# One head's V in six-row loads with 192 keys, norms that turn y as it stands, query ahead of the variance, gates in two PSUM tiles

## The chip, the cores and the metric

The kernel runs on one core of a Trainium2 chip. The metric is device time in microseconds for one execution, the median of several runs. The core has TensorE (PE in the profile, with its weight loads as PEld), VectorE (DVE), ScalarE (ACT), GpSimd (POOL) and SyncE (SP), which here issues nearly all transfers from HBM. Sixteen DMA engines carry those transfers.

## What is computed

Four decode positions (B = 4, width D = 640) go through two kinds of layer twice: attention over a cache, then a gated MLP. All data are float32.

```python
# A: W = max(256, Sk // 4) = 1024 of the 4096 cached keys, 32 heads of 128
q = (layernorm(x) @ wq) -> (B, 32, 1, 128)
p = softmax(q . k[:, :, -1024:] * 128 ** -0.5)
x = x + (p . v[:, :, -1024:]) @ wo
# B: F = 1728
gate, up = layernorm(x) @ W_gate, layernorm(x) @ W_up
x = x + (gate * (gate > 0) * up) @ W_down
# A and B once more, with the same weights and caches
```

`_layernorm` is `(x - mean) / sqrt(var + 1e-5)`, without scale or shift. Keys and values of one head are 2 x 4 x 1024 x 128 floats, 4 MB; both passes over attention need the 32 heads' K, V, query and output weights.

## The kernel before

**Memory.** One SBUF tile `store` of 50,304 columns holds everything that is loaded, as a ring that is filled by a plan made when the program is built. Host code lays weights and caches out as wide rows of 128 partitions: `heads` (most heads' q, k, o and v in the order of use), `kept` (the last two groups of heads, which stay in SBUF from the first attention to the second), `mlp`, and `limbs`. `plan` is a list of loads in order; `load()` (L226) issues the next ones on SP's queue as long as their place in `store` is free (`live`), and `done()`/`free()` mark columns as free once the products that read them are issued, and call `load()` again. A big load of `heads` has up to `MOST` = 16,064 columns, 64,256 B in each partition; three of them make a lap of the ring.

**Limbs.** V of a head is eight blocks of 512 columns (128 keys for the 4 positions each). Head 17 (`SPLIT`) has only seven in the `heads` row. The eighth block's 128 keys come in small loads of the `limbs` row: `LIMBS` (L74) lists eight loads of five rows by 1536 columns, three of two rows and two of one row by 512 columns. The rows of a load are four partitions apart. They land in the last `PART` = 2048 columns of `store`, on partitions 0 to 63. `RUNS` (L75) says which keys lie where. `stretch()` (L144) puts them into the plan: one ahead of the third last big load before the head's V, six ahead of the next and six ahead of the last. In `values()` (L463) seven small matmuls (L476) move the probabilities of those keys to the partitions where the rows landed, DVE copies them (L485), and seven matmuls with 20 or 8 rows (L490) add the products.

**Norms.** `y` is one PSUM tile that carries x through all four layers: position b of quarter g of the width stands on partition 32 g + b. `normalized()` (L376): DVE sums y (L381), ScalarE copies it to SBUF (L382), four matmuls with `sel_q` spread the mean (`mean`, L374), DVE subtracts (L385), ScalarE squares with a sum (L386), and DVE transposes in 32 x 32 blocks to `xT` (L388). `deviation()` turns the sum of squares into 1/sqrt on ScalarE and DVE (L394, L395). `query()` (L408) multiplies `xT` with one group's query weights in five parts of the width.

**MLP.** `forward()`: `gate(3)`, then gates 0 to 2 with `hidden()` and `gated()` between them, then the `down()` products into y. The gate products of all four parts go to the two halves of PSUM tile `pp`. `busy` (transposes) and `fill` (matmuls) issue work of no use for the result (L358, L365) while `waits[0]` is set, which is so in the norms and, in the first pass, through the MLP.

**Order.** The instructions of each engine run in the order of the program; nothing reorders them (`manual_schedule`). SP works its issues off in order too: an issue that waits for a place, or for the earlier DMA with its semaphore, holds those behind it.

Of the kernel before, what the change touches and what calls it, by code (L numbers as in the profile page):

```python
# [9 lines left out]
AF = mybir.ActivationFunctionType  # L10
# [63 lines left out]
LIMBS = [(half + i, 5, 0, 1536) for i in range(4) for half in (0, 32)] + [(i, 2, 1536, PART) for i in range(3)] + [(3, 1, 1536, PART), (7, 1, 1536, PART)]  # L74
RUNS = [(half, 20, 512 * s, 40 * s + 20 * (half > 0)) for s in range(3) for half in (0, 32)] + [(0, 8, 1536, 120)]  # L75


def size_of(what, i):
    if what == "v" and i == SPLIT:
        return KV - 512  # L80
    return len(HEADS[i]) * D if what == "q" else D if what == "o" else KV
# [32 lines left out]
def decode_kernel(ctx: ExitStack, tc: tile.TileContext, x, source, out):  # L114
# [29 lines left out]
    def stretch(layer, lo, end, to):  # L144

        loads = []
        for hi in fewest(lo, end, -(-(end - lo) // MOST))[1]:
            if to + hi - lo > LAP:
                to = 0
            loads.append((lo, hi, to))  # L150
            to, lo = to + hi - lo, hi
        last = next(i for i, (lo, hi, _) in enumerate(loads) if lo < at_part("v", SPLIT) + KV - 512 <= hi)
        for i, (lo, hi, at) in enumerate(loads):
            if last - 3 < i <= last:
                half = (i - last + 1) * 6 + 1
                plan.extend((layer, "limbs", p, p + 1, STORE - PART) for p in range(max(half, 0), half + 6))
            put(layer, "heads", at, lo, hi)
        return to
# [67 lines left out]
    def load():  # L226

        if not held:
            nc.sync.dma_start(out=first_q, in_=source["heads"][:, :HELD])
        while plan:  # L230
            layer, row, lo, hi, to = plan[-1]
            if any(live[to:STORE if row == "limbs" else to + hi - lo]):
                break
            plan.pop()
            if row == "limbs":
                live[to:STORE] = [lo == len(LIMBS) - 1] * PART
                p, n, a, b = LIMBS[lo]
                nc.sync.dma_start(out=store[p:p + 4 * n - 3:4, to + a:to + b], in_=source[row][p:p + 4 * n - 3:4, a:b])  # L238
                continue
            live[to:to + hi - lo] = [True] * (hi - lo)  # L240
            held.setdefault((layer, row), []).append((lo, hi - lo, to))
            nc.sync.dma_start(out=store[:, to:to + hi - lo], in_=source[row][:, lo:hi])
# [111 lines left out]
    def busy(n):  # L354

        if waits[0]:
            for _ in range(n):
                nc.tensor.transpose(po[:, :P], ident, ident)  # L358
# [18 lines left out]
    def normalized():  # L377

        ysb, xc, sq = probs[:, :QUARTER], gates[:, :QUARTER], gates[:, QUARTER:2 * QUARTER]
        waits[0] = True  # L380
        nc.vector.tensor_reduce(su, y, axis=AX.X, op=ALU.add)  # L381
        nc.scalar.copy(ysb, y)  # L382
        busy(2)
        mu = mean(su)
        nc.vector.tensor_tensor(xc, ysb, mu.to_broadcast([P, QUARTER]), op=ALU.subtract)  # L385
        nc.scalar.activation(sq, xc, AF.Square, accum_out=ss)  # L386
        fill(1)
        nc.vector.transpose(xT, xc)  # L388
        return ss
# [18 lines left out]
    def query(layer, g, spread=False):  # L408
# [7 lines left out]
        part_done(layer, "q", g, 0, (KC - 1) * n)  # L416
        c = KC - 1
# [4 lines left out]
        part_done(layer, "q", g, c * n, n)  # L422

# [39 lines left out]
    def values(layer, g, last=False):  # L463
# [3 lines left out]
        for i, h in enumerate(HEADS[g]):  # L467
# [3 lines left out]
            whole = 7 if h == SPLIT else 8  # L471
            if h == SPLIT:
                assert 0 < i < n - 1 and (layer, "limbs") not in [p[:2] for p in plan]
                limbs = bank(4 * B).rearrange("p (s x) -> p s x", s=4)
                for p, m, at, key in RUNS:
                    nc.tensor.matmul(limbs[p:p + m, at // 512], ident[:, key:key + m], to[:, 7],  # L476
                                     start=True, stop=True, tile_position=(0, p))
# [6 lines left out]
            if h == SPLIT:  # L484
                nc.vector.tensor_copy(to[:52, :4], limbs[:52])  # L485
                for p, m, first, _ in RUNS:
                    r = slice(p, p + m)
# [47 lines left out]
    def attention(layer):  # L535
        gs = order[layer]
        rstd = deviation(normalized())
        table(AF.Exp)
        query(layer, gs[0], True)
# [45 lines left out]
    def forward(layer):  # L585
# [3 lines left out]
        def gate(j):  # L589
            n, groups = (P, 4) if j < 3 else (64, 3)  # L590
            at = GU0 + j * GU if j < 3 else 0
            gus[j] = pp[:, j % 2, :2 * P]
            for c in range(KC):
                for g in range(groups):
                    lo = at + (c * groups + g) * 2 * n
                    product(gus[j][32 * g:32 * g + 32], xT[:, 32 * c:32 * c + 32], layer, "mlp", lo, 2 * n,
                            start=c == 0, stop=c == KC - 1, tile_position=(0, 32 * g))
                    done(layer, "mlp", lo, 2 * n)
# [22 lines left out]
        def down(j, last=False):  # L621
# [4 lines left out]
            for f in range(4 if j < 3 else 1):  # L626
# [10 lines left out]
                if j == 3:  # L637
                    fill(1)
                elif not (last and f > 1):
                    busy(1)  # L640
                if j == 0 and f == 1:
                    fill(2)
# [11 lines left out]
        fill(1)  # L654
        h = gated(3)
        for j, j1 in (3, 0), (0, 1), (1, 2):
            gate(j1)
            hidden(j, h)
            fill(1)
# [75 lines left out]
```

## Time and profile before

| | |
|---|---|
| time, median of 3 runs | 729.62 us (729.48 to 730.85) |
| the profiled execution | 729.74 us, span 727.9 us |
| granted TensorE clock, mean | 0.815 |
| PE busy | 450.0 us, 62% of the span |
| DVE, ACT busy | 70.5 us, 54.5 us |
| read from HBM | 310.32 MB, 426 GB/s over the span |

The profile counts from the first instruction of the program. Its DMA share is the mean busy share of the 16 DMA engines, so a share of 0.5 may be eight engines at work and eight idle. A row of the windows' view has: the stretch in us, its length, busy us and number of instructions of PE, PEld, DVE, ACT and POOL, the granted clock, the DMA share and GB/s. A row of the timeline has the start, the time, engine, line, operation and tiles, and in brackets how long the engine sat idle before it and what ended that.

### The profile page before, as it was taken

How to read it: one execution, taken by the hardware profiler on the slowest of the kernel's cores; microseconds unless marked ns; L12 is line 12 of the kernel's file. 1: busy time of each engine (PE TensorE's matmuls, PEld its weight loads, DVE VectorE, ACT ScalarE, POOL GpSimd, SP SyncE). 2: the span in 40 equal slices, each digit the busy share in tenths (PEclk: the TensorE clock that was granted, in tenths of full speed). 3: DMA queues.
4: the chain of work that ended last, by engine and by line, in shares of the span. 5: the costliest groups of instructions: out<-in, count | busy, mean ns of one | idle time of the engine just before them, and what ended most of it. 6: DMA issues, size and time to landing. Idle time of an engine off the chain costs nothing.

```text
span 727.9 us, 8368 instructions
## 1 busy us (share of the span) xinstructions
PE 450.0 (62%) x3824; PEld 146.9 (20%) x3824; DVE 70.5 (10%) x217; ACT 54.5 (7%) x102; POOL 2.4 (0%) x14
## 2 busy tenths in 40 slices
PE   3546565654645574619868896475756556558576
PEld 1111111111111121103334241021211012102123
DVE  2010001000010000001111211000000010001011
ACT  2000000000000000000412210000000000000100
POOL 0000000000000000000000000000000000000000
PEclk9567888887777787759999999677777878769989
DMA  9999999999999999999999999999999999999997
GB/s 409 444 394 447 440 444 434 412 435 444 443 428 416 421 457 418 444 422 426 418 414 412 426 431 452 429 441 433 434 423 440 438 436 417 441 444 423 425 420 312
DMA packets 13442, 310.91 MB, mean 427 GB/s; under 512 B 1576, under 2 KB 1916, under 8 KB 7136
## 3 DMA queue, kind: packets, MB, share of 16 engines
q1 hardware_dynamic: 13392, 310.37, 99.2%
q8 instruction: 30, 0.49, 0.2%
q14 instruction: 4, 0.03, 0.0%
q10 hardware_dynamic: 16, 0.01, 0.0%
HBM read 310.32 MB, written 0.05 MB: 426 GB/s over the span
## 4 chain that ended last, share of the span: by engine, by line
DMA 77%; PE 20%; DVE 1%; issue 1%; SPq 1%; ACT 0%; DVEq 0%; ACTq 0%
DMA store<-in_heads 62%; DMA store<-in_kept 9%; PE ps L276 8%; DMA store<-in_mlp 6%; PE po L276 6%; PE m L276 2%; PE y L276 1%; PE pp L276 1%; PE pp L461 1%; PE po L490 0%; PE m L432 0%; SPq L238 0%; PE po L358 0%; PE m L521 0%; PE m L512 0%
## 5 line engine op out<-in xcount | busy, mean ns | idle before, releaser
L276 PE MATMUL po<-store,pT 128*16 128x512 f32 x1026 | 157.9, 711 | 120.9 <-DMA store<-in_heads 115.2
L276 PE MATMUL ps<-store,qT 128*4 128x512 f32 (+2 forms) x998 | 152.7, 698 | 101.0 <-DMA store<-in_heads 80.7
L276 PEld LDWEIGHTS po<-store,pT 128*16 128x16 f32 x1026 | 33.4, 109 | 229.5 <-DMA store<-in_heads 126.7
L276 PEld LDWEIGHTS ps<-store,qT 128*4 128x4 f32 x998 | 30.8, 94 | 204.3 <-DMA store<-in_heads 91.8
L457 ACT ACTIVATE probs<-ps,nm 128x1024 f32<-128x1024 f32 x17 | 18.9, 1113 | 334.6 <-DVE nm L453 334.6
L453 DVE TENSOR_REDUCE nm<-ps 128x1 f32<-128x1024 f32 x17 | 20.8, 1225 | 233.9 <-PE ps L276 233.9
L276 PE MATMUL m<-store,xT 128*32 128x512 f32 (+3 forms) x146 | 27.9, 580 | 20.8 <-DMA store<-in_heads 20.8
L276 PE MATMUL y<-store,oT 128*4 128x160 f32 x512 | 23.2, 313 | 10.2 <-DMA store<-in_heads 8.9
L508 ACT COPY gates<-po 128x512 f32<-128x512 f32 x16 | 9.4, 586 | 256.5 <-PE po L276 256.5
L276 PE MATMUL pp<-store,xT 128*32 128x256 f32 (+2 forms) x320 | 20.3, 351 | 9.2 <-DMA store<-in_mlp 4.7
L470 DVE COPY pT<-pp 128x32 f32<-128x32 f32 x64 | 10.3, 184 | 143.5 <-PE po L276 126.4
L461 PE MATMUL pp<-sel_sb,probs 128*128 128x128 f32 x144 | 21.3, 297 | 0.0
L461 PEld LDWEIGHTS pp<-sel_sb,probs 128*128 128x128 f32 x144 | 18.7, 156 | 0.0
L514 DVE RECIPROCAL r<-m 128x16 f32<-128x16 f32 x18 | 4.6, 257 | 123.5 <-PE m L512 123.5
L276 PEld LDWEIGHTS y<-store,oT 128*4 128x4 f32 x512 | 12.7, 89 | 18.4 <-DMA store<-in_heads 9.2
L425 DVE TENSOR_SCALAR gates<-m,rstd 128x512 f32<-128x512 f32 (+2 forms) x18 | 12.4, 690 | 27.1 <-PE m L276 27.1
L276 PEld LDWEIGHTS pp<-store,xT 128*32 128x32 f32 x320 | 10.4, 109 | 17.7 <-DMA store<-in_mlp 8.5
L432 PE MATMUL m<-sel_sb,gates 128*128 128x128 f32 x64 | 12.7, 324 | 0.3 <-DVE gates L425 0.3
L276 PEld LDWEIGHTS m<-store,xT 128*32 128x32 f32 x146 | 6.0, 113 | 32.4 <-DMA store<-in_heads 23.3
L521 PE MATMUL m<-sel_sb,gates 128*128 128x128 f32 x72 | 11.9, 288 | 0.8 <-DVE gates L497 0.8
L432 PEld LDWEIGHTS m<-sel_sb,gates 128*128 128x128 f32 x64 | 7.9, 160 | 19.7 <-issue 18.9
L276 PE MATMUL y<-store,gates 128*4 128x160 f32 (+2 forms) x188 | 9.8, 296 | 1.7 <-DMA store<-in_mlp 1.1
(91 smaller groups left out, 135.7 us busy)
## 6 DMA issues: line engine op xcount, KB each, us to landing
store<-in_heads SPq DMA_DIRECT2D x15, 7936.0 KB
store<-in_heads SPq DMA_DIRECT2D x6, 8032.0 KB
store<-in_heads SPq DMA_DIRECT2D x2, 8000.0 KB
store<-in_heads SPq DMA_DIRECT2D x1, 7872.0 KB
store<-in_heads SPq DMA_DIRECT2D x1, 7424.0 KB
store<-in_heads SPq DMA_DIRECT2D x1, 7360.0 KB
store<-in_heads SPq DMA_DIRECT2D x1, 7168.0 KB
store<-in_heads SPq DMA_DIRECT2D x1, 6400.0 KB
```

The lines of the kernel that those rows point to most:

```text
L276: nc.tensor.matmul(out[:, a:z], by, t[rows, p:p + z - a], start=start and not a, stop=stop and z == n, **how)
L425: nc.vector.tensor_scalar(gates[:, :len(HEADS[g]) * P], qp.pop(g), rstd, SCALE, op0=ALU.mult, op1=ALU.mult)
L432: nc.tensor.transpose(qt[:, i], gates[:, i * P:(i + 1) * P], ident)
L453: nc.vector.tensor_reduce(nm[g], to.rearrange("p j n -> p (j n)"), axis=AX.X, op=ALU.max, negate=True)
L457: nc.scalar.activation(probs, sc.pop(g).rearrange("p j n -> p (j n)"), AF.Exp, bias=nm.pop(g), accum_out=sums[g])
L461: nc.tensor.transpose(pp[:, c // 4, c % 4 * P:c % 4 * P + P], probs[:, c * P:(c + 1) * P], ident)
L470: nc.vector.tensor_copy(to, pp.rearrange("p j (c x) -> p (j c) x", c=4)[:, :, i:P:32])
L508: nc.scalar.copy(gates, po)
L514: nc.vector.reciprocal(r[g], so.rearrange("p (b i) -> p i b", b=B)[:, :SIDE])
L521: nc.tensor.transpose(ot[:, 127 * b:127 * b + P], gates[:, b * P:(b + 1) * P], ident)
```

## The change

Head 17 now has six of its eight blocks in the `heads` row. The last two blocks' 256 keys come in nine small loads per layer: eight of six rows by 2048 columns on partitions 0 to 63 (192 keys), and one of 64 rows by 512 columns on partitions 64 to 127 (64 keys). Three stand ahead of each of three big loads. In `values()` nine small matmuls move probabilities for the 192 keys, one matmul on the upper 64 rows and eight on 24 rows each add the products, and one 128-row product fewer is left.

In `normalized()` DVE transposes y itself from PSUM to `xT`, one matmul spreads the mean over the transposed layout, and the mean is subtracted there from the 20 columns that hold data. The squares come from y with the mean as a bias. In `attention()` the chain of the variance is issued between the fourth and the fifth part of the first group's query. The gates alternate between the first half of `pp` and the upper half of `po`. Five of ten `busy` transposes and seven `fill` matmuls are gone from the first pass's MLP, and its gates get one `fill` where a part begins in a load of 1024 or more columns.

```diff
@@ -71,13 +71,14 @@
 FIRST, MOST = 32128, 16064
 LAP = 3 * MOST
 SPLIT, PART = 17, 2048
-LIMBS = [(half + i, 5, 0, 1536) for i in range(4) for half in (0, 32)] + [(i, 2, 1536, PART) for i in range(3)] + [(3, 1, 1536, PART), (7, 1, 1536, PART)]
-RUNS = [(half, 20, 512 * s, 40 * s + 20 * (half > 0)) for s in range(3) for half in (0, 32)] + [(0, 8, 1536, 120)]
+LIMBS = [(half + i, 6, 4, 0, PART) for i in range(4) for half in (0, 32)] + [(64, 64, 1, 0, 512)]
+RUNS = [(half, 512 * s) for s in range(4) for half in (0, 32)]
+MOVES = [(*RUNS[i], 24, 7, 24 * i) for i in range(5)] + [(*RUNS[6], 24, 6, 0), (*RUNS[7], 24, 6, 24), (*RUNS[5], 24, 6, 40), (*RUNS[5], 8, 7, 120)]
 
 
...
@@ -149,11 +150,10 @@
                 to = 0
             loads.append((lo, hi, to))
             to, lo = to + hi - lo, hi
-        last = next(i for i, (lo, hi, _) in enumerate(loads) if lo < at_part("v", SPLIT) + KV - 512 <= hi)
+        last = next(i for i, (lo, hi, _) in enumerate(loads) if lo < at_part("v", SPLIT) + KV - 1024 <= hi)
         for i, (lo, hi, at) in enumerate(loads):
             if last - 3 < i <= last:
-                half = (i - last + 1) * 6 + 1
-                plan.extend((layer, "limbs", p, p + 1, STORE - PART) for p in range(max(half, 0), half + 6))
+                plan.extend((layer, "limbs", p, p + 1, STORE - PART) for p in range(len(LIMBS)) if p // 3 == i - last + 2)
             put(layer, "heads", at, lo, hi)
         return to
 
@@ -234,8 +234,9 @@
             plan.pop()
             if row == "limbs":
                 live[to:STORE] = [lo == len(LIMBS) - 1] * PART
-                p, n, a, b = LIMBS[lo]
-                nc.sync.dma_start(out=store[p:p + 4 * n - 3:4, to + a:to + b], in_=source[row][p:p + 4 * n - 3:4, a:b])
+                p, n, by, a, b = LIMBS[lo]
+                rows = slice(p, p + by * (n - 1) + 1, by)
+                nc.sync.dma_start(out=store[rows, to + a:to + b], in_=source[row][rows, a:b])
                 continue
             live[to:to + hi - lo] = [True] * (hi - lo)
             held.setdefault((layer, row), []).append((lo, hi - lo, to))
@@ -351,11 +352,11 @@
         nc.tensor.matmul(y[32 * g:32 * g + B], ident[:B, :B], probs[:B, g * QUARTER:(g + 1) * QUARTER],
                          start=True, stop=True, tile_position=(0, 32 * g))
 
-    def busy(n):
+    def busy(n, to=po):
 
         if waits[0]:
             for _ in range(n):
-                nc.tensor.transpose(po[:, :P], ident, ident)
+                nc.tensor.transpose(to[:, :P], ident, ident)
 
 
     def fill(n, to=po):
@@ -376,16 +377,19 @@
 
     def normalized():
 
-        ysb, xc, sq = probs[:, :QUARTER], gates[:, :QUARTER], gates[:, QUARTER:2 * QUARTER]
         waits[0] = True
         nc.vector.tensor_reduce(su, y, axis=AX.X, op=ALU.add)
-        nc.scalar.copy(ysb, y)
+        nc.vector.transpose(xT, y)
         busy(2)
+        turned = bank(B)
+        nc.tensor.matmul(turned, su.to_broadcast([P, P]), sel_q[:, :B], start=True, stop=True)
         mu = mean(su)
-        nc.vector.tensor_tensor(xc, ysb, mu.to_broadcast([P, QUARTER]), op=ALU.subtract)
-        nc.scalar.activation(sq, xc, AF.Square, accum_out=ss)
+        real = xT.rearrange("p (c x) -> p c x", c=KC)[:, :, :B]
+        nc.vector.tensor_tensor(real, real, turned.unsqueeze(1).to_broadcast([P, KC, B]), op=ALU.subtract)
+        nc.vector.tensor_copy(t_sb, mu)
+        nc.scalar.activation(gates[:, :QUARTER], y, AF.Square, bias=t_sb, scale=-1.0, accum_out=ss)
+        nc.scalar.copy(probs[:, :QUARTER], y)
         fill(1)
-        nc.vector.transpose(xT, xc)
         return ss
 
     def deviation(ss):
@@ -405,7 +409,7 @@
 
     qp, nm, sums, sc, r, oT = {}, {}, {}, {}, {}, {}
 
-    def query(layer, g, spread=False):
+    def query(layer, g, spread=False, between=None):
 
 
         n = len(HEADS[g]) * P
@@ -414,12 +418,15 @@
             product(qp[g][32 * c:32 * c + 32], xT[:, 32 * c:32 * c + 32], *part(layer, "q", g, c * n, n),
                     start=True, stop=c > 0 and not spread, tile_position=(0, 32 * c))
         part_done(layer, "q", g, 0, (KC - 1) * n)
+        value = between and between()
+        turn_of[0] ^= value is not None
         c = KC - 1
         m = n // 4 if spread else n
         for a in range(n // m):
             product(qp[g][32 * a:32 * a + 32, a * m:a * m + m], xT[:, 32 * c:32 * c + 32],
                     *part(layer, "q", g, c * n + a * m, m), start=False, stop=True, tile_position=(0, 32 * a))
         part_done(layer, "q", g, c * n, n)
+        return value
 
     def query_out(g, rstd):
         nc.vector.tensor_scalar(gates[:, :len(HEADS[g]) * P], qp.pop(g), rstd, SCALE, op0=ALU.mult, op1=ALU.mult)
@@ -468,12 +475,12 @@
             t = pT[i % 2]
             to = t[:, GAP:].rearrange("p (c x) -> p c x", c=8)[:, :, :B]
             nc.vector.tensor_copy(to, pp.rearrange("p j (c x) -> p (j c) x", c=4)[:, :, i:P:32])
-            whole = 7 if h == SPLIT else 8
+            whole = 6 if h == SPLIT else 8
             if h == SPLIT:
                 assert 0 < i < n - 1 and (layer, "limbs") not in [p[:2] for p in plan]
                 limbs = bank(4 * B).rearrange("p (s x) -> p s x", s=4)
-                for p, m, at, key in RUNS:
-                    nc.tensor.matmul(limbs[p:p + m, at // 512], ident[:, key:key + m], to[:, 7],
+                for p, at, m, c, key in MOVES:
+                    nc.tensor.matmul(limbs[p:p + m, at // 512], ident[:, key:key + m], to[:, c],
                                      start=True, stop=True, tile_position=(0, p))
             for c in range(whole):
                 a = c % 4
@@ -482,9 +489,12 @@
                         start=i == 0 and c < 4, stop=i == n - 1 and c >= 4, tile_position=(0, 32 * a))
                 part_done(layer, "v", h, c * 512, 512)
             if h == SPLIT:
-                nc.vector.tensor_copy(to[:52, :4], limbs[:52])
-                for p, m, first, _ in RUNS:
-                    r = slice(p, p + m)
+                at = GAP + SIDE * B * 6 - B * i
+                nc.tensor.matmul(po[64:64 + SIDE * B], t[64:, at:at + SIDE * B], store[64:, STORE - PART:STORE - PART + 512],
+                                 start=False, stop=False, tile_position=(64, 64))
+                nc.vector.tensor_copy(to[:56, :4], limbs[:56])
+                for p, first in RUNS:
+                    r = slice(p, p + 24)
                     a = first // 512 % 2 + p // 16
                     at = GAP + SIDE * B * (first // 512) - B * i
                     nc.tensor.matmul(po[32 * a:32 * a + SIDE * B], t[r, at:at + SIDE * B],
@@ -534,9 +544,9 @@
 
     def attention(layer):
         gs = order[layer]
-        rstd = deviation(normalized())
+        ss = normalized()
+        rstd = query(layer, gs[0], True, lambda: deviation(ss))
         table(AF.Exp)
-        query(layer, gs[0], True)
         if layer:
             for t in pT:
                 nc.gpsimd.memset(t, 0.0)
@@ -589,10 +599,12 @@
         def gate(j):
             n, groups = (P, 4) if j < 3 else (64, 3)
             at = GU0 + j * GU if j < 3 else 0
-            gus[j] = pp[:, j % 2, :2 * P]
+            gus[j] = pp[:, 0, :2 * P] if j % 2 else po[:, 2 * P:]
             for c in range(KC):
                 for g in range(groups):
                     lo = at + (c * groups + g) * 2 * n
+                    if layer == 0 and j < 3 and any(lo <= a < lo + 2 * n and m >= 1024 for a, m, _ in held[0, "mlp"]):
+                        fill(1, banks[turn_of[0] ^ 1])
                     product(gus[j][32 * g:32 * g + 32], xT[:, 32 * c:32 * c + 32], layer, "mlp", lo, 2 * n,
                             start=c == 0, stop=c == KC - 1, tile_position=(0, 32 * g))
                     done(layer, "mlp", lo, 2 * n)
@@ -634,12 +646,8 @@
                             start=to is not y and f == 0, stop=f == 3 and (last or layer == j == 1 and g == 3),
                             tile_position=(0, 32 * g))
                 done(layer, "mlp", lo, D)
-                if j == 3:
-                    fill(1)
-                elif not (last and f > 1):
-                    busy(1)
-                if j == 0 and f == 1:
-                    fill(2)
+                if j < 3 and f % 2 == 0 and not (last and f > 1):
+                    busy(1, po if j else banks[turn_of[0] ^ 1])
             if j == 3:
                 for g in range(4):
                     r = slice(64 * (g // 2), 64 * (g // 2) + 64)
@@ -651,12 +659,10 @@
         waits[0] = layer == 0
         rstd = deviation(ss)
         go_on()
-        fill(1)
         h = gated(3)
         for j, j1 in (3, 0), (0, 1), (1, 2):
             gate(j1)
             hidden(j, h)
-            fill(1)
             h = gated(j1)
         down(3)
         down(0)
...
```

More of the change, by code (lines that the diff above doesn't have):

```diff
@@ L73 @@
 SPLIT, PART = 17, 2048
-LIMBS = [(half + i, 5, 0, 1536) for i in range(4) for half in (0, 32)] + [(i, 2, 1536, PART) for i in range(3)] + [(3, 1, 1536, PART), (7, 1, 1536, PART)]
-RUNS = [(half, 20, 512 * s, 40 * s + 20 * (half > 0)) for s in range(3) for half in (0, 32)] + [(0, 8, 1536, 120)]
+LIMBS = [(half + i, 6, 4, 0, PART) for i in range(4) for half in (0, 32)] + [(64, 64, 1, 0, 512)]
+RUNS = [(half, 512 * s) for s in range(4) for half in (0, 32)]
+MOVES = [(*RUNS[i], 24, 7, 24 * i) for i in range(5)] + [(*RUNS[6], 24, 6, 0), (*RUNS[7], 24, 6, 24), (*RUNS[5], 24, 6, 40), (*RUNS[5], 8, 7, 120)]
 def size_of(what, i):
     if what == "v" and i == SPLIT:
-        return KV - 512
+        return KV - 1024
     return len(HEADS[i]) * D if what == "q" else D if what == "o" else KV
@@ L698 @@
     }
-    split = parts["v"][SPLIT][:, KV - 512:]
-    parts["v"] = [v[:, :KV - 512] if h == SPLIT else v for h, v in enumerate(parts["v"])]
-    limbs = np.zeros((64, PART), np.float32)
-    for p, m, at, key in RUNS:
-        limbs[p:p + m, at:at + 512] = split[key:key + m]
+    split = parts["v"][SPLIT].reshape(P, 8, 512)
+    parts["v"] = [v[:, :KV - 1024] if h == SPLIT else v for h, v in enumerate(parts["v"])]
+    limbs = np.zeros((P, PART), np.float32)
+    for p, at, m, c, key in MOVES:
+        limbs[p:p + m, at:at + 512] = split[key:key + m, c]
+    limbs[64:, :512] = split[64:, 6]
     laid = {row: np.concatenate([parts[what][i] for what, i in row_of], axis=1) for row, row_of in PARTS.items()}
```

## The prediction

> **What bounds it now.** I read the page first: the DMA tenths, the queues and the shares of the chain that ended last.
>
> ```profile
> span 727.9 us, 8368 instructions
> ...
> DMA  9999999999999999999999999999999999999997
> ...
> DMA packets 13442, 310.91 MB, mean 427 GB/s; under 512 B 1576, under 2 KB 1916, under 8 KB 7136
> ...
> q1 hardware_dynamic: 13392, 310.37, 99.2%
> q8 instruction: 30, 0.49, 0.2%
> ...
> DMA 77%; PE 20%; DVE 1%; issue 1%; SPq 1%; ACT 0%; DVEq 0%; ACTq 0%
> ```
>
> The DMA engines are busy 99.2% of the span with the kernel's own loads. The chain still gives PE 20%, so I asked by windows whether the engines ever ran dry (columns: PE, PEld, DVE, ACT, POOL busy, granted clock, DMA share, GB/s).
>
> ```profile
> 1.70:40.00 38.30, 18.06 (x120) 5.45 (x120) 4.11 (x10) 5.04 (x8) 0.73 (x4) 0.78 1.02 433
> 40.00:340.00 300.00, 167.57 (x1260) 49.21 (x1261) 23.63 (x71) 13.31 (x23) 0.00 (x0) 0.77 1.00 433
> 340.00:390.00 50.00, 39.82 (x475) 18.55 (x473) 7.56 (x28) 11.07 (x23) 0.29 (x1) 1.00 1.01 416
> 390.00:404.00 14.00, 12.98 (x172) 5.54 (x176) 2.37 (x7) 3.53 (x10) 0.36 (x2) 1.00 1.02 403
> 404.00:720.50 316.50, 208.59 (x1744) 66.63 (x1736) 31.50 (x97) 21.30 (x40) 0.00 (x0) 0.82 1.00 433
> ```
>
> They did not: the share is 1.00 to 1.02 from 1.7 to 720.5 us (a little over 1, since neighbouring packets overlap in the record). What the chain calls PE ran while loads were still queued. So the time is a start of 1.7 us, the work of whichever of the 16 engines is last, and a tail. How uneven they are shows where they run out:
>
> ```profile
> 721.00:722.00 1.00, 0.29 (x11) 0.26 (x14) 0.00 (x0) 0.00 (x0) 0.00 (x0) 1.00 0.95 383
> 722.00:723.00 1.00, 0.98 (x32) 0.53 (x20) 0.00 (x0) 0.00 (x0) 0.00 (x0) 1.00 0.78 302
> 723.00:724.00 1.00, 0.57 (x20) 0.41 (x24) 0.33 (x1) 0.00 (x0) 0.00 (x0) 1.00 0.45 168
> 724.00:724.40 0.40, 0.40 (x16) 0.08 (x6) 0.00 (x0) 0.00 (x0) 0.00 (x0) 1.00 0.32 83
> ```
>
> Read the share as a staircase: about 15, 12, 7 and 5 of 16 engines still load. The mean engine ends at 721 + 0.95 + 0.78 + 0.45 + 0.4 x 0.32 = 723.3, the last at about 724.4. **Perfect balance would be worth 1.1 us**, 0.15% of 730. That caps what moving bytes between engines can gain, and it is less than the 0.2% (1.46 us) that a measurement of this kernel tells from no change.
>
> The execution took 729.74 us: the span and 1.84 around it. The three runs' median is 729.62 (729.48 to 730.85), so the sum below starts 0.12 above it.
>
> **The limbs.** One engine moves 433 / 16 = 27.1 GB/s. A block of V (128 rows of 2048 B) is 16,384 B an engine, 0.605 us.
>
> ```profile
> store<-in_limbs SPq DMA_DIRECT2D x16, 30.0 KB
> ...
> store<-in_limbs SPq DMA_DIRECT2D x6, 4.0 KB
> ...
> store<-in_limbs SPq DMA_DIRECT2D x4, 2.0 KB
> L238 SPq DMA_DIRECT2D store<-in_limbs x26: 249/657/842, 151.3 to 608.7; - x26
> ...
> L242 SPq DMA_DIRECT2D store<-in_heads x44: 327/328/827, 1.2 to 659.1; - x44
> L242 SPq DMA_DIRECT2D store<-in_mlp x36: 327/328/1102, 345.7 to 702.0; - x36
> L242 SPq DMA_DIRECT2D store<-in_kept x10: 327/328/436, 236.0 to 340.6; - x10
> ```
>
> How many engines share a load of n rows shows in the packets under 512 B, if these are one completion for each engine of a load: 44 + 36 + 10 big loads, `first_q` and the output on SP's queue, 92 x 16, 16 loads of five rows x 5, 6 of two x 2, 4 of one x 1, and 2 four-row transfers on ScalarE's queue x 4 make 1472 + 80 + 12 + 4 + 8 = 1576, exactly the page's count. So five rows went to five engines, a row each, and I take six rows to six. By the Trainium skill, page "DMA: Bandwidth & Descriptors", section "Why a DMA increments its semaphore by 16 and not by 1", the number of engines is the largest up to 16 that divides the rows, and they are the lowest-numbered; the count agrees with the first half, and no view here numbers engines.
>
> I call the engines of the small loads 0 to 5. Per layer, on the head's last two blocks:
> - Engines 6 to 15 had one block, 0.605; they keep four rows of the 64-row load, 8192 B, 0.303. Change **-0.30**.
> - Engines 2 to 4 had a block and eight 6144 B rows, 0.605 + 8 x 0.227 = 2.42; now 0.303 + 8 x 0.303 = 2.73. **+0.30**.
> - Engine 1 had three rows of 2048 B more (+0.23), engine 0 five (+0.38): **+0.08** and **-0.08**.
> - Engine 5 had one block; now 2.73. **+2.12**.
>
> Two layers double this. All 16 engines never stop between, so both layers count, except for an engine that runs ahead and finds nothing queued where the layers meet; there it loses its lead:
>
> ```profile
> 393.00:394.00 1.00, 1.00 (x19) 0.34 (x13) 0.00 (x0) 0.00 (x0) 0.00 (x0) 1.00 0.93 358
> ...
> 397.00:398.00 1.00, 0.94 (x31) 0.94 (x35) 0.16 (x1) 0.56 (x3) 0.00 (x0) 1.00 0.96 380
> ...
> 401.00:402.00 1.00, 1.00 (x16) 0.29 (x12) 0.00 (x0) 0.00 (x0) 0.00 (x0) 1.00 0.95 358
> ```
>
> Against the 1.02 of the whole stretch, these dips are 0.09 + 0.06 + 0.07 = some 0.2 us of the mean engine: a few early engines starve for a few us, the late ones do not. So a late engine carries both layers' change, an early one one.
>
> Which kind is last? Seven engines work after 723, and only five carry limbs, so some of the seven are relieved ones, at most 0.61 earlier. I take one of engines 2 to 4 to lie in the middle of that group, at 723.9: it ends at 723.9 + 0.6 = 724.5 and is last. **Sum: +0.1 us.** Bounds: -0.6 (no limb engine near the end) to +0.6 (a limb engine is last already).
>
> The 64-row load fills half the partitions, and no row of before shows that at speed. Below: it costs its bytes, 0.30 us an engine, as taken. Above: half the rate, 0.61 (a rival below). I take the lower, since it is nearest to the 128-row loads. By the Trainium skill, page "SBUF — State Buffer", section "Door 1: The DMA port swizzle", partitions 64 to 127 reach only half of the memory's 16 DMA ports, so this rule speaks against the load. By it the sum would be that rival's.
>
> SP issues 18 small loads for 26, some 0.66 us each, and three stand now ahead of each of three big loads. SP only has to be a load ahead: 8032 KB are 19 us of queue. Worth nothing; it would cost if a big load came 19 us late.
>
> **PE for that head.**
>
> ```profile
> L490 PE MATMUL po<-store,pT 20*16 20x512 f32 x24 | 5.5, 819 | 0.0
> L476 PE MATMUL m<-pT,sel_sb 128*20 128x4 f32 x24 | 0.6, 167 | 0.0
> L365 PE MATMUL po<-sel_sb 128*128 128x128 f32 x24 | 5.7, 328 | 0.0
> L358 PE MATMUL po<-sel_sb 128*128 128x128 f32 x18 | 5.3, 332 | 0.0
> ```
>
> A matmul shows as two records (six 20-row runs in 2 layers are 24). Two more moves and two more runs with the 64-row one are 4 x 0.17 + 4 x 0.82 = 4.0 us a layer at most, less a product saved. PE idles 108 of the 316 us of that stretch, and the DMA queue is a load deep: hidden. Uncovered it would be under 8 us.
>
> **Norms, query, gates, fillers.** Where layers meet, PE already waits for loads at the end of the down products, then the norm runs:
>
> ```profile
> 393.20 0.10 PEld L276 LDWEIGHTS y<-store,gates 128*4 128x4 f32 x4 [0.33 <-DMA store<-in_mlp]
> ...
> 394.85 0.11 PEld L276 LDWEIGHTS y<-store,gates 128*4 128x4 f32 x8 [0.26 <-DMA store<-in_mlp]
> ...
> 395.38 0.33 DVE L381 TENSOR_REDUCE ones<-y 128x1 f32<-128x160 f32 x1 [8.62 <-PE y L276]
> ...
> 396.22 0.32 DVE L385 TENSOR_TENSOR gates<-probs,m 128x160 f32<-128x160 f32 x1 [0.52 <-PE m L374]
> 396.57 0.34 DVE L388 STREAM_TRANSPOSE xT<-gates 128x160 f32<-128x160 f32 x1
> ...
> 397.14 0.50 PE L276 MATMUL m<-probs,xT 128*32 128x384 f32 x4
> ```
>
> Five busy transposes and seven fills go, 5 x 0.33 + 14 x 0.33 = 6.3 us of records; the gates gain a fill for each big load that they meet, some nine, 18 x 0.33 = 5.9. So the down products would end sooner, but the last load's landing still ends them: nothing. The new fills fall in PE's waits for the same loads (10 of 50 us idle from 340 to 390).
>
> The norm now turns y right behind the reduce, under the matmul of the mean, and subtracts 20 columns instead of 160. DVE's path from reduce to query, 0.33 + 0.32 + 0.34 and two hand-overs to 397.1, loses most of the subtract: 0.3 to 0.6 us sooner. The variance gains a copy of the mean and moves behind four fifths of the query's products; that is an added wait on PE, with the last fifth queued behind it, and query's scaling on DVE and SP's next issue wait for that. If ScalarE's square comes late, some 0.5 us go back. Splitting gates over two PSUM tiles frees PE from waits of well under 1 us. All of it only decides how early SP issues loads that no late engine waits for: between the dips refilled (0.2 us of a mean engine, none of the last) and dips 0.5 us deeper. I take nothing.
>
> **Rivals.**
> - *Relieved engines are last.* No engine of 0 to 4 lies near the end; -0.3 to -0.6 us: 729.1 to 729.4. Against it: seven late engines of 16, five with limbs. For it: 30 instruction fetches also load engines, and if the limb engines take none, the others are late.
> - *Half rate for the 64-row load.* Relieved engines gain nothing, 2 to 4 pay 0.61 a layer, 0.6 in all more than forecast: 730.4.
> - *Engine 5 is last (slower).* +2.12 us a layer, +4.24 if it carries both: from the late group up to 734.0. It decides (over 731.1) where engine 5 ended after 724.4 + 1.46 - 4.24 = 721.6, or after 723.7 if it starves at the dips. The staircase leaves room for both. Strung end to start, the trace's packets tell which strands carry limbs and which instruction fetches; some carry neither and run ahead, and I take engine 5 for one of these, though no view names it.
> - *Six rows do not go to six engines.* On two, each would carry 24 rows for 8, 16 x 0.303 = 4.8 us a layer more: 739. Against it: five rows went to five.
> - *Loads late where the layers meet.* Should the new order delay the query by several us, all engines run dry there, one for one: from 1.5 us over today's margin it is 731.2 and more. Against it: the dips are shallow and the path gets shorter.
>
> **Chances.** Forecast (729.4 to 730.2) 0.58, relieved engines last 0.12, half rate 0.17, engine 5 0.05, not six engines 0.02, late loads 0.03, and 0.03 for something that shortens start or tail. The first three are within 0.2%, with a little lost to either side: faster 0.04, same 0.88, slower 0.08. The sum is 729.74 + 0.1 = 729.8. The range 729.0 to 730.8 holds the first three cases and the scatter of runs.
>
> **What would show it.** The staircase after 720 should end at 724.1 to 724.8, steeper, with fewer engines at 722 to 723 where only leaders and engine 5 moved. 18 limb issues, and, with as many big loads as now, 1576 - 96 + 2 x (8 x 6 + 16) = 1608 packets under 512 B would show six engines; another count shows the rule wrong. Reduce to query should shrink below today's 1.76 us (395.38 to 397.14), with the share at 390 to 404 still about 1.02. A share clearly below 1 before 720 proves the premise wrong; an end past 726 with few engines left would be engine 5.

## The result and the profile after

The changed kernel takes 736.16 us (median; 734.63 to 736.39), the kernel before 729.62: a ratio of 1.0085, 95% interval 1.0073 to 1.0096. It is 6.5 us slower. The forecast was 729.8 with a range to 730.8.

The page of the changed kernel: span, DMA tenths, GB/s by slice, packets, and the queue of the loads.

```profile
span 734.4 us, 8385 instructions
...
DMA  9999999999999999999999999999999999999996
GB/s 406 440 439 402 436 440 434 440 442 422 429 438 411 417 440 434 435 425 423 408 380 378 432 428 455 429 433 436 440 426 436 437 425 435 412 432 425 428 426 279
DMA packets 13602, 310.91 MB, mean 423 GB/s; under 512 B 1608, under 2 KB 1948, under 8 KB 7200
...
q1 hardware_dynamic: 13552, 310.37, 98.9%
```

The same 310.91 MB took 6.5 us more of span at nearly the same share of busy engines (98.9% for 99.2%). The engines did not go idle much; they moved less while busy, or one of them had more to do. 1608 packets under 512 B is the count that six rows on six engines should give. The windows tell the places apart (columns as before: PE, PEld, DVE, ACT, POOL, clock, DMA share, GB/s):

```profile
40.00:340.00 300.00, 168.93 (x1261) 48.65 (x1261) 23.60 (x70) 13.15 (x22) 0.00 (x0) 0.76 1.00 431
340.00:390.00 50.00, 41.43 (x450) 19.01 (x446) 7.03 (x28) 10.58 (x22) 0.29 (x1) 1.00 0.99 400
390.00:404.00 14.00, 12.18 (x176) 5.78 (x172) 2.50 (x10) 3.86 (x9) 0.36 (x2) 0.88 0.98 367
404.00:720.50 316.50, 203.99 (x1692) 64.05 (x1688) 30.98 (x97) 21.08 (x39) 0.00 (x0) 0.81 1.00 431
726.00:727.00 1.00, 1.00 (x32) 0.64 (x24) 0.00 (x0) 0.00 (x0) 0.00 (x0) 1.00 0.88 358
727.00:728.00 1.00, 0.15 (x7) 0.00 (x0) 0.00 (x0) 0.00 (x0) 0.00 (x0) 1.00 0.71 283
728.00:729.00 1.00, 0.76 (x24) 0.66 (x28) 0.00 (x0) 0.00 (x0) 0.00 (x0) 1.00 0.56 211
729.00:730.00 1.00, 0.55 (x20) 0.18 (x16) 0.33 (x1) 0.00 (x0) 0.00 (x0) 1.00 0.16 56
730.00:731.00 1.00, 0.96 (x24) 0.45 (x24) 0.00 (x0) 0.00 (x0) 0.00 (x0) 1.00 0.12 37
```

Three things differ from before. In the two long stretches the share is still 1.00, but the rate is 431 GB/s instead of 433; over their 616 us together that is 2.9 us of transfers. Where the layers meet, 340 to 404 us, it is 400 and 367 instead of 416 and 403. And the staircase has a foot: in 730 to 731 the rate is 37 GB/s, the rate of one or two engines of 27, after the others are done.

The norm does what the prediction said of it (timeline: start, duration, engine, line, operation, output and input):

```profile
398.99 0.32 DVE L381 TENSOR_REDUCE ones<-y 128x1 f32<-128x160 f32 x1 [8.51 <-PE y L277]
399.23 0.34 DVE L382 STREAM_TRANSPOSE xT<-y 128x160 f32<-128x160 f32 x1
...
399.85 0.17 DVE L388 TENSOR_TENSOR xT<-xT,m 128x20 f32<-128x20 f32 x1 [0.28 <-PE m L385]
...
400.34 0.52 PE L277 MATMUL m<-probs,xT 128*32 128x384 f32 x4
```

From reduce to query are 1.35 us instead of 1.76.

### The profile page after: what moved, and what is told of

Its sections match the earlier page's. It is cut to its first block, busy times and chain, and to the rows that moved or that the text cites. A ratio compares the mean times of both kernels' runs of the same rounds, so it can differ in the third digit from the quotient of the medians.

```text
span 734.4 us, 8385 instructions
## 1 busy us (share of the span) xinstructions
PE 452.4 (62%) x3837; PEld 147.0 (20%) x3837; DVE 70.1 (10%) x221; ACT 54.3 (7%) x102; POOL 2.4 (0%) x14
## 2 busy tenths in 40 slices
DMA packets 13602, 310.91 MB, mean 423 GB/s; under 512 B 1608, under 2 KB 1948, under 8 KB 7200
## 3 DMA queue, kind: packets, MB, share of 16 engines
q1 hardware_dynamic: 13552, 310.37, 98.9%
## 4 chain that ended last, share of the span: by engine, by line
DMA 75%; PE 22%; another core or an unknown queue 1%; issue 1%; DVE 0%; ACT 0%; SPq 0%; DVEq 0%; ACTq 0%
DMA store<-in_heads 59%; PE ps L277 9%; DMA store<-in_kept 8%; DMA store<-in_mlp 7%; PE po L277 6%; PE m L277 2%; PE y L277 1%; PE pp L277 1%; PE pp L468 1%; PE m L439 1%; PE po L500 0%; PE m L531 0%; PE po L493 0%; PE m L522 0%
## 5 line engine op out<-in xcount | busy, mean ns | idle before, releaser
L277 PE MATMUL ps<-store,qT 128*4 128x512 f32 (+2 forms) x996 | 147.2, 675 | 96.9 <-DMA store<-in_heads 75.7
L277 PE MATMUL po<-store,xT 128*32 128x256 f32 (+2 forms) x170 | 13.8, 373 | 4.0 <-DMA store<-in_mlp 3.7
L277 PE MATMUL m<-first_q,xT 128*32 128x512 f32 (+1 forms) x42 | 7.3, 738 | 4.2 <-DMA first_q<-in_heads 2.9
```

Of the source, the lines that this page charges most:

```text
L277: nc.tensor.matmul(out[:, a:z], by, t[rows, p:p + z - a], start=start and not a, stop=stop and z == n, **how)
```

## The experiments

Differences below are against the kernel before in the same series of runs (729.52 us for the first four kernels, then 729.76, 729.72 and 729.56).

### Which half of the change costs

**old_limbs**: the changed kernel with the limbs of before, so the norm, query, gates and fillers alone.

```diff
         nc.vector.tensor_reduce(su, y, axis=AX.X, op=ALU.add)
-        nc.scalar.copy(ysb, y)
+        nc.vector.transpose(xT, y)
...
-        rstd = deviation(normalized())
+        ss = normalized()
+        rstd = query(layer, gs[0], True, lambda: deviation(ss))
```

> The changed kernel with the limbs of before (five rows, one block): the new norms, query order, gates and fillers alone. Theory A (the sixth engine of the six-row loads is already one of the late ones, and the 64-row load slows its neighbours): the time of before, 729.6, within 0.6. Rival B (the new order of norms, query, gates and fillers issues loads late where the layers meet): most of the 6.5 us stays, 734 to 736.

**new_limbs**: the kernel before with the changed limbs alone.

```diff
-LIMBS = [(half + i, 5, 0, 1536) for i in range(4) for half in (0, 32)] + [(i, 2, 1536, PART) for i in range(3)] + [(3, 1, 1536, PART), (7, 1, 1536, PART)]
+LIMBS = [(half + i, 6, 4, 0, PART) for i in range(4) for half in (0, 32)] + [(64, 64, 1, 0, 512)]
...
```

> The kernel before with the new limbs alone: six-row loads, the 64-row load, their moves and products. Theory A: 735.5 to 736.5, the whole loss. Rival B: 729.4 to 730.2.

Measured: old_limbs 729.54, ratio 0.9998 (0.9985 to 1.0012); new_limbs 735.58, ratio 1.0074 (1.0053 to 1.0095). The new limbs alone cost 6.06 us of the 6.54, the rest of the change nothing measurable: the whole loss is in the limbs. Nor does the new order of norm and query make loads late where the layers meet. There old_limbs keeps the 1.02 of before:

```profile
390.00:404.00 14.00, 12.65 (x166) 5.57 (x170) 2.29 (x8) 2.98 (x9) 0.37 (x2) 1.00 1.02 406
```

### The 64-row load and the sixth row

**no64**: the changed kernel without the 64-row load and its product (64 keys of the head are left out).

```diff
-LIMBS = [(half + i, 6, 4, 0, PART) for i in range(4) for half in (0, 32)] + [(64, 64, 1, 0, 512)]
+LIMBS = [(half + i, 6, 4, 0, PART) for i in range(4) for half in (0, 32)]
```

> The changed kernel without the 64-row load and its product: 64 of head 17's keys are left out of the result. If the load costs its bytes alone, every engine saves 0.30 us a layer: 735.5. If it also holds up the loads beside it (the staircase of the changed kernel is late by more than the bytes of the six-row loads explain, some 0.8 us a layer more), 734.0 to 734.6. If it alone is the cause of the loss, near 730.

**five_with64** and **five_no64**: the same two kernels with five rows in each of the eight loads and products of 20 rows (32 keys more are left out).

```diff
-LIMBS = [(half + i, 6, 4, 0, PART) for i in range(4) for half in (0, 32)] + [(64, 64, 1, 0, 512)]
+LIMBS = [(half + i, 5, 4, 0, PART) for i in range(4) for half in (0, 32)] + [(64, 64, 1, 0, 512)]
...
-                    r = slice(p, p + 24)
+                    r = slice(p, p + 20)
```

> The changed kernel with five rows instead of six in its eight loads and products of 20 rows; the 64-row load stays; 32 keys of the head are left out. It takes 8 x 8192 B a layer from the sixth engine, 2.42 us by the bytes. Theory that the sixth engine is late and the 64-row load holds up its neighbours: the first cost goes and the second stays, 731.3 to 732.2. Rival that the 64-row load is the whole loss: 736 as the changed kernel. Rival that the sixth engine is the whole loss: 729.5 to 730.3.

> The changed kernel with five rows instead of six in its eight loads, products of 20 rows, and without the 64-row load and its product; 96 keys of the head are left out. Theory of two causes (a late sixth engine, and a 64-row load that costs more than its bytes): both go, and 15 engines are at or under their work of before, so 729.0 to 729.7. Rival that something else in the new loads (their order, their number, their 2048 columns) costs the rest: 732 to 734, as without the 64-row load alone.

Measured, in us against before (ratio with its interval):

| | with the 64-row load | without it | the load's price |
|---|---|---|---|
| six rows | +6.54 (1.0073 to 1.0096) | +4.15 (1.0030 to 1.0062) | 2.39 |
| five rows | +1.69 (1.0012 to 1.0034) | -0.46 (0.9983 to 1.0001) | 2.15 |
| the sixth row's price | 4.85 | 4.61 | |

The two prices add up: each is nearly the same with and without the other. The sixth row costs 4.6 to 4.9 us, and its bytes, 2 x 8 x 8192 B at 27.1 GB/s, are 4.84 us of one engine. So practically every byte of the sixth rows is paid in the total time, as it would be if one engine had them all and were among the last. The 64-row load costs 2.2 to 2.4 us where its bytes are 0.6. With neither, and with 96 keys fewer, the time can't be told from before (0.46 us less, interval 1.2 less to 0.1 more): there was little to win here.

Where the sixth row is paid shows in two places of five_no64, by windows:

```profile
390.00:404.00 14.00, 12.69 (x170) 5.55 (x166) 2.29 (x8) 2.97 (x8) 0.36 (x2) 1.00 1.02 409
...
722.00:723.00 1.00, 0.55 (x19) 0.23 (x15) 0.33 (x1) 0.00 (x0) 0.00 (x0) 1.00 0.50 182
723.00:724.00 1.00, 0.85 (x28) 0.31 (x18) 0.00 (x0) 0.00 (x0) 0.00 (x0) 1.00 0.14 38
724.00:725.00 1.00, 0.51 (x8) 0.09 (x2) 0.33 (x1) 0.29 (x1) 0.00 (x0) 1.00 0.00 0
```

and of no64, which differs from it by the sixth row alone:

```profile
390.00:404.00 14.00, 11.32 (x165) 5.33 (x164) 2.30 (x8) 3.86 (x9) 0.37 (x2) 1.00 1.00 390
...
726.00:727.00 1.00, 0.57 (x20) 0.49 (x24) 0.00 (x0) 0.00 (x0) 0.00 (x0) 1.00 0.47 174
727.00:728.00 1.00, 0.70 (x24) 0.31 (x12) 0.23 (x1) 0.00 (x0) 0.00 (x0) 1.00 0.10 36
728.00:729.00 1.00, 0.85 (x24) 0.48 (x24) 0.10 (x1) 0.00 (x0) 0.00 (x0) 1.00 0.12 40
```

At the end no64 has two slices at the rate of one or two engines (36 and 40 GB/s), five_no64 one (38). Where the layers meet all engines together move 390 GB/s for 409. The reading, which no run tests by itself, is that PE can use a load only when the last engine's share has landed, so the other engines get their next work late and lose their lead there.

The trace's list of packets says more of the engine. A packet of an engine starts 3 or 4 ns before the one ahead of it ends, so from 590 us to the end the packets can be strung into 16 strands, one for each engine; limb rows and instruction fetches (packets of 16,384 B on queue q8) mark some of them. These are the times at which the strands' loads end:

| | before | before_six (below) | no64 |
|---|---|---|---|
| limb rows, no instruction fetch | five, 722.8 to 723.8 | five, 724.7 to 725.4 | five, 726.2 to 727.2 |
| limb rows and a fetch | none | one, **727.6** | one, **729.1** |
| a fetch, no limb rows | six, 723.9 to **724.4** | five, 725.3 to 727.2 | five, 725.4 to 727.0 |
| neither | five, 721.6 to 722.7 | five, 722.4 to 724.6 | five, 723.8 to 725.9 |

In the kernel before, the engines with a fetch in that window are the last ones, and none of them carries limb rows. (One fetch puts its strand back by about 1.3 us, where 16,384 B at 27.1 GB/s are 0.6.) With sixth rows one limb strand has a fetch, and it ends last. So the sixth engine is one of those six.

**before_six**: the kernel before with six rows in its eight limb loads; the sixth rows are loaded and nothing reads them. This is the sixth engine's load without anything else of the change.

```diff
-LIMBS = [(half + i, 5, 0, 1536) for i in range(4) for half in (0, 32)] + ...
+LIMBS = [(half + i, 6, 0, 1536) for i in range(4) for half in (0, 32)] + ...
```

> The kernel before, with its eight 1536-column limb loads made six rows instead of five; the sixth rows are loaded and nothing reads them. If six rows go to six engines, this puts 8 x 6144 B = 49 KB a layer on the sixth engine alone, 1.82 us by 27 GB/s, and changes no other engine. Theory that the sixth engine is one of the late ones: both layers count nearly in full, 3.4 to 3.7 us, so 732.9 to 733.3. Rival, the prediction's own assumption that the sixth engine runs ahead and has slack: at most 0.3 us, 729.5 to 729.9. Rival that the after kernel's loss is all from the 64-row load: 729.5 as well.

Measured: 733.08, +3.32, ratio 1.0047 (1.0032 to 1.0062). Its packets and its end, by the page and by windows:

```profile
DMA packets 13474, 311.01 MB, mean 425 GB/s; under 512 B 1592, under 2 KB 1932, under 8 KB 7168
```

```profile
726.00:727.00 1.00, 0.55 (x19) 0.23 (x15) 0.33 (x1) 0.00 (x0) 0.00 (x0) 1.00 0.13 51
727.00:728.00 1.00, 0.90 (x30) 0.37 (x18) 0.00 (x0) 0.00 (x0) 0.00 (x0) 1.00 0.14 35
```

1592 is 1576 plus one completion for each of 16 loads, so one engine more takes part and carries the 3.64 us by itself. 3.32 of 3.64 are paid (2.3 to 4.5 by the interval). An engine with slack would have swallowed its slack first: by the medians the sixth engine ended some 0.3 us before the last one in the kernel before, at about 724.1, which lies among the 723.9 to 724.4 of the six strands with fetches. 0.1 MB of 311 on the wrong engine cost half a per cent.

### What the 64-row load does beside its bytes

**before_add64**: the kernel before plus such a load (it lands in free rows, nothing reads it), as the last limb load.

```diff
-... + [(3, 1, 1536, PART), (7, 1, 1536, PART)]
+... + [(3, 1, 1536, PART), (7, 1, 1536, PART)] + [(64, 64, 0, 512)]
...
-range(max(half, 0), half + 6))
+range(max(half, 0), half + 6 + (i == last)))
```

> The kernel before, plus one load of 64 rows of 512 columns a layer into partitions 64 to 127, which nothing reads: 131 KB a layer, 0.30 us of each of 16 engines by the bytes. If it costs its bytes: 0.6 us in all, 730.2. If it moves at half rate: 1.2 us, 730.8. Theory that it also holds up the packets of the loads beside it on the other engines: 1.8 to 2.5 us, 731.4 to 732.0.

Measured: 737.66, +7.90, ratio 1.0110 (1.0093 to 1.0127), far above every expectation, and no clean test. Its SP timeline:

```profile
216.30 3.96 SPq L238 DMA_DIRECT2D store<-in_limbs  x7
236.32 0.35 SPq L243 DMA_DIRECT2D store<-in_heads  x1
```

In the kernel before, six limb loads go out here and the big load follows at once:

```profile
216.11 3.35 SPq L238 DMA_DIRECT2D store<-in_limbs  x6
219.57 0.36 SPq L242 DMA_DIRECT2D store<-in_heads  x1
```

Behind seven small loads the big one is issued 16 us later, and the engines run dry before it comes:

```profile
234.00:236.00 2.00, 0.00 (x0) 0.00 (x0) 0.00 (x0) 0.00 (x0) 0.00 (x0) 0.50 0.20 69
```

The waits' view puts this on an earlier `heads` load. The clean test has no more than six small loads between two big ones. Three kernels, all the kernel before with loads that nothing reads, ahead of the first limb load:

**add64_high**: 64 rows on partitions 64 to 127. **add64_mid**: the same on partitions 32 to 95. **add64_twice**: two loads on partitions 64 to 127.

```diff
-LIMBS = [(half + i, 5, 0, 1536) ...
+LIMBS = [(64, 64, 1536, PART)] + [(half + i, 5, 0, 1536) ...
...
-                half = (i - last + 1) * 6 + 1
+                half = (i - last + 1) * 6 + 2
```

(For add64_mid 32 stands for the first 64; add64_twice has `(64, 64, 1024, 1536)` as well, and + 3.)

> The kernel before, plus one load a layer of 64 rows of 512 columns into partitions 64 to 127, ahead of the first limb loads, so that no more than six small loads stand between two big ones; nothing reads it. By the bytes 0.6 us in all, 730.2. Theory that a load of one half of the partitions holds up its neighbours: 1.6 to 2.5 us, 731.3 to 732.2. Rival that the 7.9 us of the earlier run with such a load are its own price, and not the wait behind seven small loads: 736 to 738.

> The kernel before, plus one load a layer of 64 rows of 512 columns into partitions 32 to 95, ahead of the first limb loads; nothing reads it. The same bytes as a load into partitions 64 to 127, but half of them in each half of the partitions. Theory that a 64-row load is dear because it fills one half only: here it costs its bytes, 0.6 us in all, 730.2 to 730.6. Rival that it is dear because it is one more load with four small packets an engine: 731.3 to 732.3, as the load into partitions 64 to 127.

> The kernel before, plus two loads a layer of 64 rows of 512 columns into partitions 64 to 127, ahead of the first limb loads; nothing reads them. By the bytes 1.2 us in all, 730.9. If each load holds up its neighbours by itself: twice the cost of one, 3.2 to 5 us, 732.9 to 734.7. If two in a row share one hold-up: 732.0 to 732.8.

Measured: add64_high 732.85, +3.13 (1.0027 to 1.0057); add64_mid 731.09, +1.37 (1.0006 to 1.0025); add64_twice 735.80, +6.08 (1.0066 to 1.0096). Same bytes, same number of packets (13602 in both), same place in the order: where the rows lie makes 1.8 us. It is mainly the half of the partitions that is dear, not the extra load, and it is dear in proportion: two cost 6.08, one 3.13. add64_mid came 0.5 to 0.9 us above its expectation; its interval, 0.4 to 1.8 us, still holds the 0.6 of its bytes.

How that looks in a profile: the load of the second layer passes at 580 to 590 us. Windows of add64_high, then of add64_mid:

```profile
580.00:590.00 10.00, 0.83 (x8) 0.11 (x8) 0.00 (x0) 0.00 (x0) 0.00 (x0) 0.53 1.03 402
```

```profile
580.00:590.00 10.00, 3.10 (x19) 0.95 (x22) 1.15 (x2) 0.00 (x0) 0.00 (x0) 0.50 1.01 434
```

The engines count as busy in both (1.03 and 1.01), but move 402 instead of 434 GB/s. 7% of 10 us is 0.7 us of all 16 engines, in one layer. Ten us are short for such a reading, since a packet of 63,488 B alone takes 2.34 us. The packets themselves settle it: in add64_high 28 large ones (40,000 B or more) between 583.8 and 591.5 us take up to 1.36 times their 27.1 GB/s time, 0.9 us too much on the mean of the 16 engines, and 23 in the first layer 0.6 us. In add64_mid only single packets are too long, 18 of 20 of them beside an instruction fetch. So the load slows the packets beside it; with its own bytes that is 2.1 of the 3.13 us. A full share says that the engines hold packets, not that they move at their rate.

### The sixth rows elsewhere

**sixth_spread**: the changed kernel with five-row loads, and the sixth rows in two loads of four neighbouring rows on partitions 20 to 23 and 52 to 55 (all rows are loaded).

```diff
-LIMBS = [(half + i, 6, 4, 0, PART) for i in range(4) for half in (0, 32)] + [(64, 64, 1, 0, 512)]
+LIMBS = [(half + i, 5, 4, 0, PART) for i in range(4) for half in (0, 32)] + [(half + 20, 4, 1, 0, PART) for half in (0, 32)] + [(64, 64, 1, 0, 512)]
...
-... if p // 3 == i - last + 2)
+... if p // 4 == i - last + 2)
```

> The changed kernel with the sixth rows of the eight six-row loads taken out and loaded as two four-row loads: the same bytes, but the sixth engine carries none of them and four of the first five carry two rows more (0.6 us a layer). Theory A: the sixth engine loses 2.4 us a layer and no longer sets the end; the engines behind it and the 64-row load remain: 732 to 733.5. Rival B, or the 64-row load as the only cause: 736 as before.

Measured: 737.02, +7.50 (1.0059 to 1.0121). A miss: the rows left the sixth engine, and nothing was won. Its end by windows:

```profile
728.00:729.00 1.00, 1.00 (x32) 0.67 (x27) 0.00 (x0) 0.00 (x0) 0.00 (x0) 1.00 0.68 249
729.00:730.00 1.00, 0.55 (x20) 0.32 (x16) 0.33 (x1) 0.00 (x0) 0.00 (x0) 1.00 0.27 99
730.00:731.00 1.00, 0.88 (x27) 0.28 (x17) 0.00 (x0) 0.00 (x0) 0.00 (x0) 1.00 0.05 19
```

The lone engine at the foot is gone (0.05 instead of 0.12), but in 728 to 729 more engines still load (0.68 instead of 0.56). All became later. The suspicion was the four-row loads themselves, so:

**add4**: the kernel before plus these two loads, which nothing reads, ahead of the first limb load.

```diff
-LIMBS = [(half + i, 5, 0, 1536) ...
+LIMBS = [(20, 4, 0, PART), (52, 4, 0, PART)] + [(half + i, 5, 0, 1536) ...
...
-                half = (i - last + 1) * 6 + 1
+                half = (i - last + 1) * 6 + 3
```

> The kernel before, plus two loads a layer of four neighbouring rows of 2048 columns, into partitions 20 to 23 and 52 to 55, ahead of the first limb loads; nothing reads them. They put 2 x 8192 B a layer on four engines, 0.6 us each by the bytes, 1.2 in both layers. If they cost their bytes: 0.6 to 1.2 us, 730.3 to 730.9. Theory that four neighbouring rows hold up the engines beside them, which would explain why spreading the sixth rows gained nothing: 732 to 735.

Measured: 734.87, +5.31, ratio 1.0073 (1.0056 to 1.0090). By bytes it is at most 1.2. The same reading as for the 64 rows, by windows of add4:

```profile
580.00:590.00 10.00, 0.69 (x6) 0.00 (x0) 0.00 (x0) 0.00 (x0) 0.00 (x0) 0.79 0.99 395
```

395 GB/s at a share of 0.99. By packets, 23 large ones between 585.9 and 593.0 us take up to 2.1 times the time of their bytes. 5.31 us on top of five_with64's +1.69 make 7.0 of sixth_spread's 7.50.

The sixth rows lay on the same partitions, 20 to 23 and 52 to 55, in the changed kernel too. So sixth_spread by itself leaves open whether their engine or their partitions make them dear. The packets speak for the engine: in no64 and before_six the limb rows take the time of their bytes, and no group of large packets beside them is slowed. There the sixth rows cost because they stand in the line of an engine that is last. No run puts them on another engine and on other partitions as well, so whether that would make them cheap is not shown.

By the Trainium skill, page "SBUF — State Buffer", section "Door 1: The DMA port swizzle", partitions 64 to 127 are reached through 8 of 16 ports, 32 to 95 through all, and 20 to 23 and 52 to 55 through one and the same, at about 27 GB/s a port. An estimate from that page: 65,536 B a layer through one port are 2.4 us, 4.8 in both layers, for the 5.31 of add4; 131,072 B through 8 ports are 0.6 a layer, 1.2 in both, for the 2.2 to 3.1 measured with 64 rows. Order and direction agree; for the 64-row load the price by that rate is too small.

## Why the prediction was wrong

**The bound held.** The DMA engines set the time; PE, SP's fewer issues, the norm, the query, the gates and the fillers were taken as nothing, and old_limbs says +0.02 us.

**Six rows on six engines held**: 1608 packets, as forecast.

**The step that failed is the choice for engine 5.** The prediction worked out +2.12 us a layer for it, saw that the staircase left room for both cases, and decided: "some carry neither and run ahead, and I take engine 5 for one of these". It was in the late group: before_six puts it some 0.3 us from the last engine, at about 724.1, far behind the 721.6 from which the rival decides. There are engines that carry neither limb rows nor fetches and run ahead, five of them (721.6 to 722.7); engine 5 is not one of them, but one of the six with instruction fetches and no limb rows. With that, the prediction's own +4.24 us give the rival's upper end, 734.0; measured for the sixth row are 4.6 to 4.9. The rival with a chance of 0.05 was the main event, 70 to 74% of the loss. The error was not of arithmetic but of identity: of eleven strands without limb rows six were late, so to take engine 5 for one of the other five needed a reason, and none was given. The one load that sat on a single engine should have widened the range to its full price.

**The second term was mis-sized.** "Below: it costs its bytes, 0.30 us an engine, as taken. Above: half the rate, 0.61." The upper end was not one. Taken alone the load's price is 2.15 to 2.39 us in the changed kernel, that is 1.1 to 1.2 a layer, nearly twice the upper bound and nearly four times the value taken. What was missing is that such a load also slows the packets of the loads beside it (up to 1.37 times in the changed kernel, 58 large packets in both layers); a bound from the load's own bytes can't contain that.

**Premise.** "All 16 engines never stop between" held up to 340 us (share 1.00). Where the layers meet it held less than before: 0.98 instead of 1.02 in 390 to 404. The cause that the prediction looked for, a query that comes late, is excluded by old_limbs (1.02). What makes the dip are the sixth rows: the changed kernel without them (five_with64, first line) is back at 406 GB/s instead of 367, and the kernel before with them (before_six, second line) falls to 372 from 403.

```profile
390.00:404.00 14.00, 12.16 (x167) 5.46 (x170) 2.30 (x8) 3.75 (x9) 0.37 (x2) 1.00 1.01 406
```

```profile
390.00:404.00 14.00, 12.93 (x178) 5.96 (x180) 2.37 (x7) 3.91 (x9) 0.36 (x2) 1.00 0.99 372
```

**The cap.** Perfect balance would be worth 1.1 us, said the prediction, so nothing large could be won; that held, as five_no64 with less to load gained 0.46. But a cap on the gain is no cap on the loss: an engine that is already last pays in full.

**The rivals.** "Six rows do not go to six engines" fell. "Relieved engines are last" was near the truth for the kernel before, with the reason that it gave, the instruction fetches: the six strands that end last there carry no limb rows. Its time still fell, since one of these engines was engine 5 and was not relieved. The prediction's limb engine in the late group, taken at 723.9, is there as well (723.8). "Half rate" was right in its direction and named the right load.

Open: which of the six late strands is engine 5 in the kernel before, since neither views nor packets number engines; and by what mechanism the 64-row load costs about twice what half the rate would.

## What to carry to other kernels

When all DMA engines are busy to the end, the time is that of the last engine, not of the bytes: for each small load work out which engines take it, and take every engine to be last until a run with a few dummy rows on it, or the trace's packets, say otherwise. In these runs a small load was cheapest with its rows in both halves of the partitions or four partitions apart, and dear in one half or on neighbours; its own bytes were not its price. And read GB/s beside the DMA share, since a share of 1.03 at 402 GB/s is a loss that the share hides.

## What the runs showed of the hardware that was not expected

- A load of 128 KB into partitions 64 to 127 cost 1.5 to 1.6 us (3.13 for two, 6.08 for four), the same bytes into partitions 32 to 95 0.7 (1.37 for two).
- Two loads of 32 KB into partitions 20 to 23 and 52 to 55 cost 2.7 us a layer, more than 128 KB on half of the partitions.
- An instruction fetch of 16,384 B put its engine back by about 1.3 us, and the six engines with fetches after 590 us were the last ones in the kernel before.
- With seven small loads ahead of a big one, the big one was issued 16 us later than with six, and some 4.8 us (7.90 less the 3.13 of add64_high) went to engines that ran dry. That the count of seven is the reason is inferred: in this kernel the load's columns and its place differ as well.
